# Issuing the second of two down-projection matmuls without its own weight load

## The chip, the cores and the metric

The kernel runs on one core of one Trainium2 chip. The metric is the device time of one execution in microseconds. (The granted clock is the share of full speed at which TensorE was allowed to run.)

## The reference

One transformer block with adaptive layer norm: linear attention, then a SwiGLU feed-forward network. Only the feed-forward part matters here. It has 2048 tokens, width D = 1024 and hidden width F = 3584, all in bfloat16.

```python
def _B_ref(x, w_gate, w_up, w_down):
    g = _silu(x @ w_gate)
    u = x @ w_up
    return g * u @ w_down            # [2048, 3584] @ [3584, 1024]: the down projection
# ...
x = x + gb * _B_ref(h, B_w_gate, B_w_up, B_w_down)
```

## The kernel before

The kernel records every operation in a list with its engine and its dependencies, and emits all engines' programs at the end. So nearly every instruction of the profile carries the line of the same helper (L176), and one tells groups apart by their tiles: `gug` and `guu` are gate and up weights, `wd_a` and `wd_b` are two parts of the down weights, `at` holds the activations g * u, `ps` is PSUM.

A multiplication on TensorE has two operands, a stationary one (`lhsT`, 128 x 128 in the down projection) and a moving one (`rhs`, 128 x 512). One `matmul` call of the kernel leaves two records in the profile, 4147 of each in before: an LDWEIGHTS of the stationary tile on "PEld", called the weight load here, and a MATMUL on "PE".

```python
for ch in range(NCH):                                   # 4 chunks of 512 tokens
    for ft in range(NFT):                               # 28 tiles of the hidden width
        # ...
        for dt in range(NDT):                           # 8 gate matmuls, each with its own weights
            P.pe("matmul", out=PS[:, gbank, :], lhsT=GUG[slot][:, dt, ftl * 128:(ftl + 1) * 128],
                 rhs=H2T[:, dt, :], start=(dt == 0), stop=(dt == NDT - 1))
        # ... the same eight for up with GUU; silu, product into AT
    for j in range(4):                                  # 4 row tiles of 128 tokens
        st = 4 * ch + j
        bb = 4 + 2 * (st % 2)
        last = st == NST - 1
        if not last:
            for ft in range(NFT):
                for nh in range(2):                     # two halves of the output, same lhsT
                    P.pe("matmul", out=PS[:, bb + nh, :], lhsT=AT[:, ft, j * 128:(j + 1) * 128],
                         rhs=WD(ft)[:, nh * 512:nh * 512 + 512], start=(ft == 0), stop=(ft == NFT - 1))
        # ... the last row tile has its own order; eviction, residual, output
```

In the innermost loop both halves `nh` have the same stationary tile, and before the change that tile is loaded for each of them (56 loads for the 56 matmuls of a row tile, in the timelines below).

## Time and profile before

| | before |
|---|---|
| device time, median of 3 runs | 834.54 us (834.38 to 834.56) |
| profiled span | 832.1 us |
| PE (matmul) busy | 825.8 us, 99% |
| PEld (weight load) busy | 380.1 us, 46%, 4147 loads |
| start to start of 512-column down matmuls | 215.8 ns |

Some lines of the page of before follow: busy time by engine (busy us, share of the span, count), the granted clock in 40 slices (9 is 90% or more), the chain of work that ended last by engine and by line, and four groups of instructions (line, engine, operation, output<-inputs, shapes, count | busy us, mean ns of one | idle time of the engine before them and what ended it).

```profile
PE 825.8 (99%) x4147; PEld 380.1 (46%) x4147; DVE 302.8 (36%) x662; ACT 196.3 (24%) x335; POOL 43.2 (5%) x56
...
PEclk9999999999999999999999999999999999999999
...
PE 97%; DVE 2%; DMA 0%; issue 0%; POOL 0%; ACT 0%; DVEq 0%
PE ps L176 97%; DVE stats L176 0%; DVE xres L176 0%; DMA xres<-in_A_x_dram 0%; DVE acc L176 0%; DVE mhl L176 0%; DVE ve L176 0%; POOL rstd L176 0%; DVE mv L176 0%; ACT mw L176 0%; DVE ut L176 0%; DVE mean L176 0%; DVE msq L176 0%; DVE nmr L176 0%; DVE sumx L176 0%
...
L176 PE MATMUL ps<-wd_a,at 128*128 128x512 bf16 (+2 forms) x528 | 113.5, 373 | 0.0
...
L176 PE MATMUL ps<-wd_b,at 128*128 128x512 bf16 (+2 forms) x396 | 85.8, 373 | 0.0
L176 PEld LDWEIGHTS ps<-wd_a,at 128*128 128x128 bf16 x528 | 51.1, 98 | 59.8
...
L176 PEld LDWEIGHTS ps<-wd_b,at 128*128 128x128 bf16 x396 | 38.3, 98 | 44.7
```

The chain shows what a gain must come from: 97% of the span is matmul following matmul. The groups must be read with care. The mean of 379 ns (373 where narrower forms are mixed in) is the reported duration of one matmul, but the matmuls of this stage start 215.7 ns apart, so their records overlap. Their cost here is the distance between starts, and the timeline gives that. Here is the timeline of PE in before around the start of the first down stage: start us, length us, engine and line, what, count.

```profile
345.97 7.07 PE L176 MATMUL ps<-wd_a,at 128*128 128x512 bf16 x32
352.87 5.34 PE L176 MATMUL ps<-wd_b,at 128*128 128x512 bf16 x24
358.05 7.07 PE L176 MATMUL ps<-wd_a,at 128*128 128x512 bf16 x32
```

A row tile of the down stage is 56 matmuls (32 + 24). It starts at 345.97 us and the next one at 358.05: 12.08 us / 56 = 215.7 ns. The timeline of PEld in before for the same stretch shows where the loads lie:

```profile
345.75 6.79 PEld L176 LDWEIGHTS ps<-wd_a,at 128*128 128x128 bf16 x32
352.66 5.06 PEld L176 LDWEIGHTS ps<-wd_b,at 128*128 128x128 bf16 x24
357.84 6.79 PEld L176 LDWEIGHTS ps<-wd_a,at 128*128 128x128 bf16 x32
```

The load for the matmul that starts at 345.97 us starts at 345.75, one matmul earlier, and takes 0.098 us. The loads for 352.87 and 358.05 lead by the same amount. So it is in all of the stage: each of its 224 loads starts 1 or 2 ns after the start of the matmul before its own, and ends before the recorded end of that matmul.

### The profile page before, as it was taken

To read this page: it belongs to the slowest core of one execution; us is meant where nothing else is said; L and a number is where in the kernel's file an instruction comes from. 1 tells how busy PE (TensorE), PEld (TensorE's weight loads), DVE (VectorE), ACT (ScalarE), POOL (GpSimd) and SP (SyncE) were. 2 spreads that over 40 slices of the span, in tenths; PEclk is the share of its full clock that TensorE was granted. 3 is DMA by queue.
4 is the path that set the end of the run, shared out by engine and by line. 5 is a ranking of instruction groups with operands and counts; after the bars stand their busy time and mean duration, and the time that the engine had idled before them with its cause. 6 is when DMAs were issued, how large, how long until landed. Compare 5 with 4: busy or idle time off the path is not lost.

```text
span 832.1 us, 10139 instructions
## 1 busy us (share of the span) xinstructions
PE 825.8 (99%) x4147; PEld 380.1 (46%) x4147; DVE 302.8 (36%) x662; ACT 196.3 (24%) x335; POOL 43.2 (5%) x56
## 2 busy tenths in 40 slices
PE   8999999999999999999999999999999999999998
PEld 4544444454444444444444444444444444444444
DVE  5797985657873222120221111122111212111111
ACT  3767642222332111110111111111111111111011
POOL 1000000000050000030000003000000300000000
PEclk9999999999999999999999999999999999999999
DMA  9969734928287885710455571045558004553000
GB/s 320 289 149 232 217 60 148 200 102 302 41 220 245 261 258 152 185 44 13 114 152 152 152 193 35 13 117 151 153 152 195 30 13 120 153 153 94 1 26 25
DMA packets 190924, 117.17 MB, mean 141 GB/s; under 512 B 49560, under 2 KB 174624, under 8 KB 190880
## 3 DMA queue, kind: packets, MB, share of 16 engines
q1 hardware_dynamic: 190864, 116.55, 51.5%
q8 instruction: 32, 0.52, 0.3%
q14 instruction: 12, 0.10, 0.0%
q10 hardware_dynamic: 16, 0.00, 0.0%
HBM read 100.67 MB, written 4.33 MB: 126 GB/s over the span
## 4 chain that ended last, share of the span: by engine, by line
PE 97%; DVE 2%; DMA 0%; issue 0%; POOL 0%; ACT 0%; DVEq 0%
PE ps L176 97%; DVE stats L176 0%; DVE xres L176 0%; DMA xres<-in_A_x_dram 0%; DVE acc L176 0%; DVE mhl L176 0%; DVE ve L176 0%; POOL rstd L176 0%; DVE mv L176 0%; ACT mw L176 0%; DVE ut L176 0%; DVE mean L176 0%; DVE msq L176 0%; DVE nmr L176 0%; DVE sumx L176 0%
## 5 line engine op out<-in xcount | busy, mean ns | idle before, releaser
L176 PE MATMUL ps<-h2t,gug 128*128 128x512 bf16 x896 | 211.7, 379 | 0.0
L176 PE MATMUL ps<-h2t,guu 128*128 128x512 bf16 x896 | 211.7, 379 | 0.0
L176 DVE TENSOR_TENSOR at<-sg,ps 128x512 bf16<-128x512 bf16 x112 | 77.0, 688 | 296.1 <-PE ps L176 296.1
L176 ACT ACTIVATE sg<-ps 128x512 bf16<-128x512 f32 x112 | 66.9, 597 | 310.3 <-PE ps L176 310.3
L176 PEld LDWEIGHTS ps<-h2t,guu 128*128 128x128 bf16 x896 | 87.7, 98 | 105.7
L176 PEld LDWEIGHTS ps<-h2t,gug 128*128 128x128 bf16 x896 | 87.5, 98 | 105.3
L176 PE MATMUL ps<-wd_a,at 128*128 128x512 bf16 (+2 forms) x528 | 113.5, 373 | 0.0
L176 PE MATMUL ps<-ht,wqk 128*128 128x512 bf16 x512 | 112.1, 379 | 0.1
L176 PE MATMUL ps<-wd_b,at 128*128 128x512 bf16 (+2 forms) x396 | 85.8, 373 | 0.0
L176 PEld LDWEIGHTS ps<-wd_a,at 128*128 128x128 bf16 x528 | 51.1, 98 | 59.8
L176 PEld LDWEIGHTS ps<-ht,wqk 128*128 128x128 bf16 x512 | 49.3, 98 | 58.4 <-issue 0.2
L176 DVE TENSOR_TENSOR ut<-att,gb_b 128x512 bf16<-128x512 bf16 (+1 forms) x32 | 14.4, 450 | 166.7 <-ACT att L176 166.7
L176 ACT ACTIVATE att<-ps 128x512 bf16<-128x512 f32 (+1 forms) x32 | 17.4, 591 | 182.1 <-PE ps L176 182.1
L176 PEld LDWEIGHTS ps<-wd_b,at 128*128 128x128 bf16 x396 | 38.3, 98 | 44.7
L176 PE MATMUL ps<-pk,xres 128*128 128x512 bf16 x256 | 56.7, 379 | 0.0
L176 PE MATMUL ps<-mw,pqt 128*128 128x512 bf16 x256 | 56.2, 379 | 0.1
L176 POOL TENSOR_SCALAR h2t<-h2t,modcol 128x512 bf16<-128x512 bf16 x32 | 28.4, 901 | 395.2 <-DMA h2t<-xn 378.8
L176 ACT ACTIVATE e<-ps 128x512 bf16<-128x512 f32 x56 | 33.2, 604 | 32.3 <-PE ps L176 24.1
L176 PEld LDWEIGHTS ps<-mw,pqt 128*128 128x128 bf16 x256 | 24.9, 98 | 29.7 <-DVE xres L176 0.2
L176 PEld LDWEIGHTS ps<-pk,xres 128*128 128x128 bf16 x256 | 24.8, 98 | 29.8 <-issue 0.4
L176 ACT ACTIVATE junk<-xres 128x1024 bf16<-128x1024 bf16 x24 | 25.4, 1058 | 36.0 <-DVE xres L176 35.8
L176 POOL TENSOR_TENSOR rstd<-ve,neghalf 128x1 f32<-128x1 f32 (+2 forms) x17 | 14.1, 842 | 214.9 <-DVE ve L176 174.8
(101 smaller groups left out, 343.7 us busy)
## 6 DMA issues: line engine op xcount, KB each, us to landing
gug<-in_B_w_gate_dram SPq DMA_DIRECT2D x56, 512.0 KB, 4.0
guu<-in_B_w_up_dram SPq DMA_DIRECT2D x56, 512.0 KB, 5.3
xres<-in_A_x_dram SPq DMA_DIRECT2D x20, 256.0 KB, 8.1
rb<-recip_den SPq DMA_DIRECT2D x8, 512.0 KB, 11.9
stgx<-in_w_mod_dram SPq DMA_DIRECT2D x2, 2048.0 KB, 7.9
wd_a<-in_B_w_down_dram SPq DMA_DIRECT2D x4, 1024.0 KB, 7.3
out_dram<-xres SPq DMA_DIRECT2D x31, 128.0 KB, 1.7
xres<-in_A_x_dram SPq DMA_DIRECT2D x3, 1024.0 KB, 12.9
```

The lines of the kernel that those rows point to most:

```text
L176: return getattr(e, method)(**kw)
```

## The change

The intent is to stop loading a tile that is already there. A helper builds the matmul instruction with its own weight load switched off, and the down projection uses it for `nh == 1`. In 15 row tiles of 28 tiles that takes away 420 of 4147 loads. The order of matmuls, the data and the synchronisation are the same.

```diff
--- before.py
+++ after.py
@@ -117,6 +117,14 @@
 _WRITE_KEYS = ("out", "accum_out", "ap")
 
 
+def _matmul_held(e, out, lhsT, rhs, start, stop):
+    bass_ = e.bass
+    return e.add_instruction(mybir.InstMatmult(
+        name=bass_.get_next_instruction_name(), engine=mybir.EngineType.PE, start_tensor_calc=start,
+        stop_tensor_calc=stop, tile_size=(128, 128), tile_position=(0, 0), ldweights=False,
+        ins=[e.lower_ap(rhs), e.lower_ap(lhsT)], outs=[e.lower_ap(out)]))
+
+
 class _Prog:
     COMPUTE = ("pe", "act", "dve", "pool")
 
@@ -173,7 +181,7 @@
         kw = dict(kw)
 
         def fn(e, method=method, kw=kw):
-            return getattr(e, method)(**kw)
+            return _matmul_held(e, **kw) if method == "matmul_held" else getattr(e, method)(**kw)
 
         return self.add(eng, fn, reads, writes, lane=lane, tag=tag or method)
 
@@ -1124,7 +1132,7 @@
                 if not last:
                     for ft in range(NFT):
                         for nh in range(2):
-                            P.pe("matmul", out=PS[:, bb + nh, :], lhsT=AT[:, ft, j * 128:(j + 1) * 128],
+                            P.pe("matmul_held" if nh else "matmul", out=PS[:, bb + nh, :], lhsT=AT[:, ft, j * 128:(j + 1) * 128],
                                  rhs=WD(ft)[:, nh * 512:nh * 512 + 512], start=(ft == 0), stop=(ft == NFT - 1))
                 for nh in range(2):
                     i = nh
```

## The prediction

> **What bounds the kernel now.** TensorE's matmul stream. The chain of waits gives 97% of the 832.1 us span to matmuls; the busy table has PE at 825.8 us (99%), VectorE at 302.8, ScalarE at 196.3. The per-core view shows a mean granted clock of 1.000. The waits of PE sum to under 4 us.
>
> The changed stage is the down projection. In the timeline, its first 56 matmuls (one row tile) start at 345.97 us and the next row tile at 358.05: 215.7 ns from start to start. The whole first chunk, 224 matmuls, runs from 345.97 to 394.31 us, 215.8 ns each. The reported 379 ns of one matmul is overlapped with its neighbours; it is not what a matmul costs here. Gate and up, where every matmul really needs new weights, run at the same pace (8 in 1.73 us).
>
> [...]
>
> **What the change removes.** 15 row tiles x 28 contraction tiles = 420 of the 4147 weight loads (the last row tile keeps its own). Each is 98 ns by the groups table: 41 us of PEld busy time. Nothing is added; matmuls, order, banks, semaphores and data are the same.
>
> **How much lies on the critical path.** None that I can see. The load for the matmul at 345.97 starts at 345.75: one matmul period ahead. It takes 98 ns of that 216 and is done some 118 ns before it is needed. The load before 358.05 shows the same lead (357.84). [...] I expect 0 to 0.3 us.
>
> A loss would need the next tile's load to be unable to run ahead of the held matmul. Fully exposed, 420 x 98 ns = 41 us, 5% slower. Unlikely: the load has two matmuls, 431 ns, to hide under.
>
> **Predicted time: 834.4 us, range 832.5 to 836.0.** Faster by over 2%: 0.01. Within 2%: 0.96. Slower by over 2%: 0.03.
>
> **What would show each step right or wrong.** PEld instructions drop from 4147 to 3727, PEld busy from 380 to about 339 us; matmul count stays at 4147. The down stage's starts stay at 215.7 ns, chunk one at 48.3 us. PE's share of the chain stays at 97%. Remaining loads keep 98 ns and start before the preceding held matmul ends. [...] If matmuls after a remaining load start late, the load lost its overlap.
>
> **What would make it wrong.** A held matmul that is handled differently from one with its own load; a load that cannot pass a held matmul; a lower granted clock. A weight-load busy share 5 points lower is not evidence of a gain.

The sum of the forecast is the 834.54 us of before less the expected 0 to 0.3 us, of which the middle gives 834.4. The 0 rests on the loads that are done 118 ns early; the 0.3 us is the author's estimate.

## More of the kernel before

Last, a window over the first down stage of before (from:to, length, then busy us and count of PE, PEld, DVE and ACT, granted clock, DMA share, GB/s). PE has no idle time in it, and loads lie under 45% of it (21.91 of 48.33 us):

```profile
345.97:394.30 48.33, 48.33 (x225) 21.91 (x224) 0.69 (x1) 3.25 (x6) 1.00 0.23 60
```

## The result

| | before | after |
|---|---|---|
| device time, median (4 runs each) | 834.54 us | 834.39 us (834.25 to 834.46) |
| PEld busy, loads | 380.1 us, 4147 | 338.9 us, 3727 |
| PE busy, matmuls | 825.8 us, 4147 | 825.9 us, 4147 |
| first down stage, first to last start (224 matmuls) | 48.131 us | 48.131 us |

The ratio is 0.9999, with a 95% interval of 0.9985 to 1.0013: no change that could be told from noise.

Lines of the page of after that answer to those of before. The held matmuls have a line of their own, L122, because another helper makes them; all else has moved from L176 to L184.

```profile
PE 825.9 (99%) x4147; PEld 338.9 (41%) x3727; DVE 302.1 (36%) x662; ACT 196.3 (24%) x335; POOL 43.2 (5%) x56
...
PEclk9999999999999999999999999999999999999999
...
PE 97%; DVE 2%; DMA 0%; POOL 0%; issue 0%; ACT 0%; DVEq 0%
PE ps L184 87%; PE ps L122 11%; DVE stats L184 0%; DVE xres L184 0%; DMA xres<-in_A_x_dram 0%; DVE acc L184 0%; DVE mhl L184 0%; DVE ve L184 0%; POOL rstd L184 0%; DVE mv L184 0%; ACT mw L184 0%; DVE ut L184 0%; DVE mean L184 0%; DVE msq L184 0%; DVE nmr L184 0%
...
L184 PE MATMUL ps<-wd_a,at 128*128 128x512 bf16 (+2 forms) x288 | 98.4, 367 | 0.0
L122 PE MATMUL ps<-wd_a,at 128*128 128x512 bf16 x240 | 91.0, 379 | 0.0
...
L184 PE MATMUL ps<-wd_b,at 128*128 128x512 bf16 (+2 forms) x216 | 73.9, 367 | 0.0
...
L122 PE MATMUL ps<-wd_b,at 128*128 128x512 bf16 x180 | 68.2, 379 | 0.0
L184 PEld LDWEIGHTS ps<-wd_a,at 128*128 128x128 bf16 x288 | 27.6, 98 | 82.6 <-issue 79.1
...
L184 PEld LDWEIGHTS ps<-wd_b,at 128*128 128x128 bf16 x216 | 20.7, 98 | 62.3 <-issue 60.1
```

Weight loads lost 41 us of busy time. The chain is still 97% matmul (87% and 11% on the two lines), and the reported duration of a held matmul is still 379 ns. The same window over the first down stage, in after:

```profile
345.97:394.30 48.33, 48.33 (x226) 11.05 (x113) 0.69 (x1) 3.33 (x7) 1.00 0.24 60
```

PEld busy is halved, 21.91 to 11.05 us, and PE is as full as before. (The counts include matmuls that only overlap the edges of the window. In after the stage starts 0.15 us earlier, so the last 0.15 us of this window belong to the next stage.) A short piece of the timeline of after shows the new pattern, with matmuls that load (L184), held ones (L122) and loads (PEld):

```profile
357.90 0.38 PE L184 MATMUL ps<-wd_a,at 128*128 128x512 bf16 x1
358.12 0.38 PE L122 MATMUL ps<-wd_a,at 128*128 128x512 bf16 x1
358.12 0.10 PEld L184 LDWEIGHTS ps<-wd_a,at 128*128 128x128 bf16 x1 [0.33 <-issue]
358.33 0.38 PE L184 MATMUL ps<-wd_a,at 128*128 128x512 bf16 x1
```

Matmuls start at 357.90, 358.12 and 358.33: the pace is the same whether a load belongs to the matmul or not. Over the first three chunks, the trace has on average 215.8 ns from a loaded matmul to a held one and 215.8 ns back, in after, and exactly the same two means between first and second matmuls in before. The remaining loads lead their matmuls by 0.21 to 0.22 us, as before: the load at 358.12 starts with the held matmul and serves the matmul at 358.33. It uses one matmul of time to hide in, not the two that the change gives it.

### The profile page after: what moved, and what is told of

Read it like the earlier page. It is cut to its first block, busy times and chain, and to the rows that moved or that the text cites. A ratio compares the mean times of both kernels' runs of the same rounds, so it can differ in the third digit from the quotient of the medians.

```text
span 832.0 us, 9719 instructions
## 1 busy us (share of the span) xinstructions
PE 825.9 (99%) x4147; PEld 338.9 (41%) x3727; DVE 302.1 (36%) x662; ACT 196.3 (24%) x335; POOL 43.2 (5%) x56
## 4 chain that ended last, share of the span: by engine, by line
PE 97%; DVE 2%; DMA 0%; POOL 0%; issue 0%; ACT 0%; DVEq 0%
PE ps L184 87%; PE ps L122 11%; DVE stats L184 0%; DVE xres L184 0%; DMA xres<-in_A_x_dram 0%; DVE acc L184 0%; DVE mhl L184 0%; DVE ve L184 0%; POOL rstd L184 0%; DVE mv L184 0%; ACT mw L184 0%; DVE ut L184 0%; DVE mean L184 0%; DVE msq L184 0%; DVE nmr L184 0%
## 5 line engine op out<-in xcount | busy, mean ns | idle before, releaser
L184 PE MATMUL ps<-h2t,gug 128*128 128x512 bf16 x896 | 211.7, 379 | 0.0
L184 PE MATMUL ps<-h2t,guu 128*128 128x512 bf16 x896 | 211.7, 379 | 0.0
L184 DVE TENSOR_TENSOR at<-sg,ps 128x512 bf16<-128x512 bf16 x112 | 77.0, 687 | 296.2 <-PE ps L184 296.2
L184 ACT ACTIVATE sg<-ps 128x512 bf16<-128x512 f32 x112 | 66.9, 597 | 310.3 <-PE ps L184 310.3
L184 PEld LDWEIGHTS ps<-h2t,guu 128*128 128x128 bf16 x896 | 87.7, 98 | 105.7
L184 PEld LDWEIGHTS ps<-h2t,gug 128*128 128x128 bf16 x896 | 87.5, 98 | 106.0 <-issue 1.0
L184 PE MATMUL ps<-ht,wqk 128*128 128x512 bf16 x512 | 112.2, 379 | 0.1
L184 PE MATMUL ps<-wd_a,at 128*128 128x512 bf16 (+2 forms) x288 | 98.4, 367 | 0.0
L122 PE MATMUL ps<-wd_a,at 128*128 128x512 bf16 x240 | 91.0, 379 | 0.0
L184 DVE TENSOR_TENSOR ut<-att,gb_b 128x512 bf16<-128x512 bf16 (+1 forms) x32 | 13.7, 429 | 167.4 <-ACT att L184 167.4
L184 PE MATMUL ps<-wd_b,at 128*128 128x512 bf16 (+2 forms) x216 | 73.9, 367 | 0.0
L184 PEld LDWEIGHTS ps<-ht,wqk 128*128 128x128 bf16 x512 | 49.2, 98 | 58.6 <-DVE ht L184 0.6
L122 PE MATMUL ps<-wd_b,at 128*128 128x512 bf16 x180 | 68.2, 379 | 0.0
L184 PEld LDWEIGHTS ps<-wd_a,at 128*128 128x128 bf16 x288 | 27.6, 98 | 82.6 <-issue 79.1
L184 ACT ACTIVATE att<-ps 128x512 bf16<-128x512 f32 (+1 forms) x32 | 17.4, 591 | 182.1 <-PE ps L184 182.1
L184 PE MATMUL ps<-pk,xres 128*128 128x512 bf16 x256 | 56.7, 379 | 0.0
L184 PE MATMUL ps<-mw,pqt 128*128 128x512 bf16 x256 | 56.2, 379 | 0.1
L184 POOL TENSOR_SCALAR h2t<-h2t,modcol 128x512 bf16<-128x512 bf16 x32 | 28.4, 902 | 394.9 <-DMA h2t<-xn 378.6
L184 PEld LDWEIGHTS ps<-wd_b,at 128*128 128x128 bf16 x216 | 20.7, 98 | 62.3 <-issue 60.1
L184 ACT ACTIVATE e<-ps 128x512 bf16<-128x512 f32 x56 | 33.2, 604 | 32.4 <-PE ps L184 22.3
L184 PEld LDWEIGHTS ps<-mw,pqt 128*128 128x128 bf16 x256 | 24.9, 98 | 29.7 <-DVE xres L184 0.2
L184 PEld LDWEIGHTS ps<-pk,xres 128*128 128x128 bf16 x256 | 24.7, 98 | 29.8 <-issue 0.4
## 6 DMA issues: line engine op xcount, KB each, us to landing
xres<-in_A_x_dram SPq DMA_DIRECT2D x3, 1024.0 KB, 13.3
```

The source lines that it names most:

```text
L122: return e.add_instruction(mybir.InstMatmult(name=bass_.get_next_instruction_name(), engine=mybir.EngineType.PE, start_tensor_calc=start, ...
L184: return _matmul_held(e, **kw) if method == "matmul_held" else getattr(e, method)(**kw)
```

## The experiments

Two questions were left. Is the weight load really hidden because it runs beside the matmul before it, or is a load free for some other reason? And how much could a load cost, where would holding the weights pay? Each kernel below is the one before or after with a small edit. All results were correct except in e1. In the first four runs (one chip) before measured 834.76 us, in the next four 834.75, in the last 834.74.

### e1: hold the weights in gate and up as well

```diff
-  P.pe("matmul", out=PS[:, gbank, :], ...)
+  P.pe("matmul_held" if dt else "matmul", out=PS[:, gbank, :], ...)
   # and the same for ubank
```

> The kernel after, with seven of every eight gate and up matmuls held as well: 1568 more weight loads gone. The result is wrong on purpose (seven tiles of eight are multiplied by the wrong weights); the stream of matmuls is the same. Theory A (a load of 98 ns runs under the matmul before it, 216 ns, and costs nothing): weight-load busy falls from 339 to about 185 us and the time stays within 0.2% of the kernel before; starts stay 215.8 ns apart. [...] Rival C (the change did save, and something else took it back in the down stage only): gate and up would show the saving, up to 98 ns a load.

Measured: 834.47 us, ratio 0.9995 (0.9978 to 1.0012). The busy times of this run:

```profile
PE 826.2 (99%) x4147; PEld 186.0 (22%) x2159; DVE 302.2 (36%) x662; ACT 196.2 (24%) x335; POOL 43.3 (5%) x56
```

Weight-load busy fell from 380 to 186 us and nothing was gained: 1988 loads fewer than before, and a measured difference of 0.3 us, inside the noise. Held gate and up matmuls start 215.8 ns apart like the others. A stretch of gate and up, 80 us of after and then of e1 (columns as in the windows above, with POOL after ACT), has PE full in both and PEld down from 36.30 to 5.06 us:

```profile
260.00:340.00 80.00, 80.00 (x387) 36.30 (x386) 17.90 (x29) 13.73 (x23) 0.00 (x0) 1.00 0.79 228
```

```profile
260.00:340.00 80.00, 80.00 (x386) 5.06 (x63) 17.83 (x30) 13.73 (x23) 0.00 (x0) 1.00 0.80 230
```

The result was wrong (relative error 0.157), so a held matmul does use the tile that was loaded before it. All this rules out Rival C. It also speaks against Rival B: that swapping the weights takes a part of each matmul's time. By an estimate from the starts of before and e5 (see e5), 2.5 ns of a matmul could be such a part; 1988 times that would be 5.0 us, and the interval allows 1.8 us at most (0.22% of 834.76). Theory A is left.

### e2: four loads for each down matmul

```diff
+  for _ in range(3):
+      P.pe("ldweights", weights=AT[:, ft, j * 128:(j + 1) * 128])
   P.pe("matmul", out=PS[:, bb + nh, :], ...)
```

> The kernel before, with three extra loads of the same weight tile ahead of each of the 840 down matmuls of the first 15 row tiles: four loads per matmul. If a load holds its path for the whole 98 ns that the profile shows, four take 392 ns, more than the 216 ns of a matmul: starts 392 ns apart, +148 us. If 98 ns is a latency and loads follow each other faster (the matmuls with one moving column start 25 ns apart in the trace of before, each with its own load), four take about 100 ns, still hidden: starts 216 ns, +0 us. If loads cost the stream anything at all when hidden, the time grows in proportion to 2520 loads.

Measured: median 835.24 us, ratio 1.0008 (0.9993 to 1.0023). One of four runs took 837.02 us, with a mean granted clock of 0.998 where the other three had 1.000; it was not profiled, so its cause is open. The profiled one took 834.42 us; starts in its trace stay 215.8 ns apart. A piece of the timeline, with the three extra loads as one row (0.18 us) and the matmul's own load after it (0.10 us):

```profile
350.35 0.18 PEld L176 LDWEIGHTS <-at 128*128 128x128 bf16 x3
350.47 0.10 PEld L176 LDWEIGHTS ps<-wd_a,at 128*128 128x128 bf16 x1
```

Each group of three takes 0.18 us although one load takes 0.096 us, so loads overlap: in the trace they start 40 to 42 ns apart (350.134, 350.176 and 350.216 us for one group of three, 350.256 us for the matmul's own). So 98 ns is the time from start to end of one load, not the time for which it keeps others out. Four of them fit under one matmul. This run quadruples the loads of the stage, where e1 took loads away, and the time again does not follow.

### e3 and e4: no load may run ahead

In both, each down matmul waits for the semaphore of the matmul before it. e3 makes the edit in before, e4 makes it in after.

```diff
+  if ft or nh:
+      P.wait_for("pe", [prev_mm])
-  P.pe(..., out=PS[:, bb + nh, :], ...)
+  prev_mm = P.pe(..., out=PS[:, bb + nh, :], ...)
```

> The kernel before, but in the down stage every matmul, and so its load, waits for the semaphore of the matmul before it, so that no load can run ahead. To be read against e4_serial_held. By itself: starts at least 379 ns (the reported latency) apart plus the way over the semaphore and the load; estimate 500 to 550 ns, so the time grows by 240 to 280 us.

> The kernel after with the same waits as e3_serial_own: the second of two matmuls has no load. Theory A (what hid the load was that it ran ahead): a held matmul starts about 93 ns sooner than one with its load, the amount by which the trace of before has matmuls late where a load starts only with its own matmul (309 ns apart in place of 216); 420 x 93 = 39 us less than e3. Rival D (a load costs nothing even then, because a matmul may stream while its weights still arrive, or a held matmul pays for something else): no difference, within 4 us.

Measured: e3 1028.02 us, e4 1020.98 us; the difference is 7.0 us, or 17 ns for each of 420 held matmuls. This lies between both forecasts of e4: not 39 us, not within 4. In the estimate of 500 to 550 ns for e3, the 379 and the 98 ns are from the trace of before; the rest was allowance for the semaphore, which no run had shown. The growth of e3, 193 us, is below the forecast 240 to 280, since starts are 450 ns apart and not 500 to 550. Two loads in the timeline of e3, each with the idle time before it and what ended it:

```profile
350.31 0.10 PEld L176 LDWEIGHTS ps<-wd_a,at 128*128 128x128 bf16 x1 [0.35 <-PE ps L176]
350.76 0.10 PEld L176 LDWEIGHTS ps<-wd_a,at 128*128 128x128 bf16 x1 [0.35 <-PE ps L176]
```

and of e4, where L122 is held:

```profile
350.25 0.10 PEld L184 LDWEIGHTS ps<-wd_a,at 128*128 128x128 bf16 x1 [0.79 <-PE ps L122]
350.25 0.39 PE L184 MATMUL ps<-wd_a,at 128*128 128x512 bf16 x1
350.70 0.38 PE L122 MATMUL ps<-wd_a,at 128*128 128x512 bf16 x1
351.13 0.10 PEld L184 LDWEIGHTS ps<-wd_a,at 128*128 128x128 bf16 x1 [0.79 <-PE ps L122]
```

In e3 each load now waits for the previous matmul and starts 450 ns after the load before it. In e4 a held matmul follows a loaded one by 447 ns and a loaded one follows a held one by 437 ns: 884 ns for two in place of 900. So a load does cost something once it can't run ahead, but 16 ns, not 98. The trace shows why: the matmul starts 4 ns after the start of its load (load at 350.310 us in e3, matmul at 350.314) instead of after its end, and its reported duration is 390 ns in place of 376 for a held one (such ends are modelled; the 16 ns come from starts alone). How matmul and load run together in that time, the trace doesn't show.

The 93 ns of the expectation came from places in before where a matmul starts 309 ns after the previous one and 4 ns after its own load. I had misread them. Before has five such places, and at four the load comes with a semaphore wait (for example at 23.537 and 134.529 us), so the distance holds a wait and is not the price of a load; at the fifth (121.875 us) the stationary tile changes its width, from 128 to 8, which was not studied. Where a late load in before belongs to a matmul of 512 columns that others follow freely (for example the one at 193.106 us), the next matmul comes 226 or 227 ns later instead of 216: 10 ns, of the size that e3 and e4 show.

### e5 and e6: 128 columns, with and without loads

e5 cuts the 840 down matmuls into pieces of 128 columns, each with a load; e6 holds seven of the eight pieces that share a tile.

```diff
-  P.pe("matmul", out=PS[:, bb + nh, :], lhsT=..., rhs=WD(ft)[:, nh * 512:nh * 512 + 512], start=(ft == 0), ...)
+  for c0 in range(0, 512, 128):
+      P.pe("matmul",                                   # e6: "matmul_held" if nh or c0 else "matmul"
+           out=PS[:, bb + nh, c0:c0 + 128], lhsT=..., rhs=WD(ft)[:, nh * 512 + c0:nh * 512 + c0 + 128],
+           start=(ft == 0 and c0 == 0), ..., skip_group_check=True)
```

> The kernel before, with every down matmul of the first 15 row tiles cut into four of 128 columns, each with its own load: four times the loads, less work to hide each one. Before's trace has 128-column matmuls with their own loads 56 ns apart, and e2 has loads following each other 40 ns apart. Theory A2 (a load needs its path for about 40 ns, 98 ns is only its latency): starts 56 ns apart, 4 x 56 - 216 = 8 ns more for each former matmul, 840 x 8 = +6.5 us. If 98 ns were the pace of loads: 98 ns apart, +148 us.

> The same cut, but seven of the eight pieces that share a weight tile are held (2940 loads gone against e5). Theory A2: starts 56 ns apart as in e5, same time within 1 us. If a load at this size costs anything, e6 is faster than e5 by 2940 times that cost; 98 ns loads: 126 us.

Measured: e5 841.18 us, e6 841.40 us, 6.4 and 6.7 us over before; the forecast was 6.5 for e5 and the same within 1 us for e6. The busy times of e5, then of e6, show the loads that are gone:

```profile
PE 832.8 (99%) x6667; PEld 485.9 (58%) x6667; DVE 302.6 (36%) x662; ACT 196.2 (23%) x335; POOL 43.2 (5%) x56
```

```profile
PE 833.9 (99%) x6667; PEld 339.5 (40%) x3727; DVE 303.0 (36%) x662; ACT 196.5 (23%) x335; POOL 43.2 (5%) x56
```

Starts are 55.83 ns apart on average over the first down stage in both. With 215.83 ns at 512 columns this gives (215.83 - 55.83) / 384 = 0.4167 ns for a column, and 2.5 ns for each matmul beside its columns, an estimate from these two widths. The starts are the same with and without loads at both widths (55.83 ns in e5 and e6, 215.8 in before and after), so the 2.5 ns isn't the swapping of weights. Had it been, the change would have saved 420 x 2.5 ns = 1.0 us.

### e7 and e8: 32 columns, with and without loads

The same cut with 32 columns, in the first four row tiles only: 3584 matmuls in the place of 224.

> The kernel before, with every down matmul of the first four row tiles cut into sixteen of 32 columns, each with its own load: 3584 matmuls[...]. If a load needs its path for 40 ns, as where loads follow each other in e2, starts are 40 ns apart and the stage grows by 3584 x 40 - 224 x 216 ns = +95 us. If the 25 ns that one-column matmuls with loads showed is the pace: +41 us.

> The same cut with 31 of the 32 pieces held. Theory A2 (at this size the load is no longer hidden): [...] faster than e7 by at least 15 ns for each of 3472 held matmuls, 52 us or more. Rival E (the matmul itself has a floor of 25 ns whether it loads or not, and a load fits into it): the same time as e7 within 1%, both at 25 ns. A negative result here means that holding weights pays at no width in a stream that runs freely.

Measured: e7 889.47 us, e8 876.16 us. The typical distance between starts is 25 ns in both (3226 of 3583 in e7, 3378 in e8, to the nanosecond of the record), so Rival E holds for the stream: a load fits even into 25 ns. Theory A2 falls at this width: it said 40 ns for e7 and 52 us or more between e7 and e8 (3472 times the 15 ns from 25 to 40). The loads of e7 themselves start 25 ns apart, so the 40 ns of e2 is not a time for which every load keeps its path. In e7, 32 pieces in a row load the same tile, but that is not the reason: in before, the 64 matmuls of one column with `siluc` and `wca` have a different tile each, and most of their starts (58 of 63), and of their loads (55 of 63), are 25 ns apart too. e8's growth of 41.4 us is what 3584 x 25 - 224 x 215.8 ns, 41.3 us, says. But e7 is 1.5% slower than e8, more than Rival E said, so the null that would have spoken against holding at every width was not found. The windows over the stage, e7 first (the columns are those of the windows above, with POOL after ACT):

```profile
346.30:448.90 102.60, 93.80 (x3582) 91.60 (x3581) 5.61 (x13) 3.88 (x7) 6.01 (x8) 0.98 0.14 32
```

```profile
346.50:436.00 89.50, 89.50 (x3584) 10.55 (x111) 5.52 (x13) 3.34 (x7) 6.02 (x8) 1.00 0.14 35
```

In e8, PE is busy throughout. In e7, PE is idle for 8.8 of 102.60 us; in distances between starts the loss is 13.1 us, and 12.9 us of it is 27 single gaps, 16 of them of 277 to 279 ns, one of 2.4 us, each exactly 128 matmuls after the one before (for example at 369.869, 373.322 and 376.776 us). With loads, 128 matmuls are 256 instructions. Here are the ends of the two longest gaps, with the idle time before each and no releaser but "issue":

```profile
354.96 3.56 PE L185 MATMUL ps<-wd_a,at 128*128 128x32 bf16 x128 [2.24 <-issue]
359.24 3.71 PE L185 MATMUL ps<-wd_a,at 128*128 128x32 bf16 x132 [0.72 <-issue]
```

The granted clock was 0.50 from 354.89 to 358.30 us, from the end of the longest gap on, which makes the 0.98 of the stage and the 0.998 of the run. Matmuls started 26.7 ns apart there, so this cost 0.2 us; it does not explain the rest.

The DMA queue that carries instructions (packets, MB, share of 16 engines) shows in e7 and in e8:

```profile
q8 instruction: 59, 0.97, 0.4%
```

```profile
q8 instruction: 44, 0.72, 0.3%
```

One packet is 0.97 MB / 59 = 16 KB. The 7507 matmuls and 7507 loads of e7 are 254 for each of the 59 packets, close to the 256 between gaps. The same division gives 259 in before (8294 by 32 packets), 254 in after (7874 by 31), 252 in e1 (6306 by 25) and 262 in e8 (7507 matmuls and, by its edit, 4035 loads, by 44). What a packet holds, no view shows; that it is some 256 instructions is an estimate from these counts. It would fit a wait for the instruction stream, which e7 would use at one packet in 3.2 us (128 x 25 ns, an estimate) and e8 at about half that rate. The kept trace has the times of each packet, and they point the same way: 27 instruction packets start in this stage of e7, one for each gap, and each gap ends 1.2 to 1.6 us after such a packet has landed. In e8 the packets come some 6 us apart in most of the stage, and no two matmuls start more than 28 ns apart. That is a tie in time; no run changed the instruction stream alone. If it is the cause, what a load cost here was room in the instruction stream, not time beside the matmuls. At 512 columns no such gap appears in the first down stage of before: no two neighbours start more than 216 ns apart.

### e9: ten loads for each down matmul

The edit is that of e2 with `range(9)`.

> The kernel before, with nine extra loads of the same weight tile ahead of each of the 840 down matmuls of the first 15 row tiles: ten loads per matmul. In e2 the loads followed each other 40 ns apart, the first of them 2 ns after the start of the matmul before, and four of them fitted. Theory A2 (a load runs beside the matmul stream on a path of its own that it holds for about 40 ns): ten take about 400 ns, more than the 216 ns of a matmul, so starts are 400 ns apart or a little more, and the time grows by at least 840 x 184 ns = 155 us. Rival F (a load of a tile that is already there, or that is followed by another load, is skipped and costs nothing, so that e2 proved nothing): starts stay 216 ns apart, +0 us.

Measured: 969.49 us, +134.75 us; starts are 376.7 ns apart. A piece of the timeline (nine extra loads in one row, then the matmul's own):

```profile
352.15 0.42 PEld L176 LDWEIGHTS <-at 128*128 128x128 bf16 x9
352.51 0.10 PEld L176 LDWEIGHTS ps<-wd_a,at 128*128 128x128 bf16 x1
```

The window over its first down stage has PE and PEld both busy in all of it:

```profile
346.10:430.10 84.00, 84.00 (x224) 84.00 (x2232) 5.52 (x13) 3.26 (x6) 6.01 (x8) 1.00 0.14 36
```

So loads of a tile that is already there are not free, Rival F falls, and e2's null is a true one. The size is 13% below the forecast of at least 155 us, which counted ten full steps of 40 ns: the trace has nine (362 ns), then, as in e3, the matmul starts 4 ns after its last load, and the next load 11 ns after that. 362 + 4 + 11 = 377. The row of loads becomes the limit somewhere between four and ten loads for one matmul. Why loads in a row start 40 ns apart, where those of e7, with a matmul between them, start 25 ns apart, stays open: e9 does not tell a limit of the loads themselves from the pace at which loads in a row are issued.

No run points to a version that beats both kernels. The stream of matmuls is the limit, and no experiment shortened it.

## Why the prediction was right

The forecast was that nothing would change, and nothing that could be told from noise did. That 834.4 us was met within 0.01 us is luck: runs of one kernel differ by 0.2 us here, and by more in later rounds (834.48 to 835.13 us for before).

**The bound.** Right. The chain is 97% matmul in both traces and the stage's starts are 215.8 ns apart in both, to the nanosecond over 224 matmuls. In neither trace do any two matmuls of 512 columns start less than 215 ns apart.

**What is removed.** Right: 420 loads, 41 us of PEld busy time, and nothing else.

**How much is on the critical path.** Right: none. e1 removed 4.7 times as many loads and gained nothing, e2 added 2520 and lost nothing that the trace shows, and e9 shows that loads take time which appears in the total once there are too many to fit beside a matmul. That is the mechanism by experiment from both sides: in before and after the load (98 ns) runs beside the matmul before its own, starting 1 or 2 ns after it.

**The swapping of weights.** A passage that is cut from the prediction left a small gain for it. The runs show none: starts don't alternate in after (215.8 ns both ways), and e5 and e6 have the same 55.83 ns.

**The size of the possible loss.** Mis-sized. The prediction costed a load that is fully exposed at 98 ns, 41 us for 420. e3 and e4 show 16 to 17 ns, 7 us, because a matmul starts 4 ns after its late load starts. Also "the load has two matmuls, 431 ns, to hide under" was wrong in its detail: in after it still starts one matmul ahead, with the held one. Neither touched the time, because neither is on the path.

**The share of weight-load time.** The prediction did not count its fall as a gain. It was 46%, 41% and 22% in before, after and e1, at 834.54, 834.39 and 834.47 us, so that was right.

## What to carry to other kernels

Before removing an instruction, look where its time lies: compare the start of each load with the start of the matmul before it, and the distance between matmul starts with that of a stretch that can't avoid the loads. Here the pace was the same with and without, 215.8 ns, and 41 us of removed busy time were worth nothing that could be told from noise. Holding weights paid where loads couldn't run ahead (16 ns each, e3 and e4) and perhaps where the instructions were too many (e8 took 13.3 us less than e7, with matmuls 25 ns apart). It did not pay in a free stream of matmuls of 512 columns (after, e1) or of 128 (e6). Widths other than 512, 128 and 32 were not run.
